# Pinned buffer homes and a later sink-key copy in a windowed-attention and feed-forward kernel

## The chip, the cores and the metric

The kernel runs on one core of one Trainium2 chip. The metric is the device time of one launch in microseconds (us). Each kernel was run several times; the text gives medians and ranges. Medians and ranges take every run; ratios take the runs counted as fast (at most 1.5% above the fastest of their kernel). Engines are named as in the profile: PE is TensorE (PEld its weight loads), DVE is VectorE, ACT is ScalarE, POOL is GpSimd, SP is SyncE.

## The reference, cut to what matters

Four batches of attention (8 heads, 768 positions, head size 64) in which each query sees the first 4 positions (the "sinks") and a window of 128 positions; then a multiplicative feed-forward over all 3072 rows.

```python
keep = is_sink | in_window              # 4 sink keys, or the last 128 keys
a = softmax(where(keep, q @ k.T / 8, -1e9))
x = (a @ v) reshaped to (3072, 512)
out = ((x @ w1) * (x @ w2)) @ w3 @ w_out
```

## The kernel before: the parts that matter

Every per-batch buffer is declared for four batches, with two, three or four physical homes under one tag. Which home a batch gets is decided when the program is built, by what is free then.

```python
def per_batch(name, shape, bufs):
    return [inp.tile(shape, BF16, tag=name, bufs=bufs, name=f"{name}{b}") for b in range(B)]

qN = per_batch("qN", [P, NB, DM], 2)      # queries as loaded
kN = per_batch("kN", [P, NB, DM], 2)      # keys as loaded
vN = per_batch("vN", [P, NB, H, VS], 3)
qT = per_batch("qT", [P, NP, S], 2)       # queries transposed
kT = per_batch("kT", [P, NP, S], 2)       # keys transposed
ksbd = per_batch("ksbd", [P, 648], 4)     # the 4 sink keys of all heads, spread out
# ... (cut)
```

Batches 0 and 1 are transposed on TensorE, batches 2 and 3 by DMA (6 key tiles and 6 query tiles each, issued from SP). The sink keys are two tiny VectorE copies out of the first key tile, and the sink scores are a TensorE product that needs those copies and the transposed queries:

```python
def sink_keys(b):
    for e in range(2):
        hp = slice(64 * e, 64 * e + 64)
        kk = ksbd[b][hp, 4 * e:4 * e + 640].rearrange("p (r x) -> p r x", x=160)
        nc.vector.tensor_copy(kk[:, :, 0:4], kT[b][hp, :, 0:4])
    yield

def sink_scores(b, t):
    sp = ps_mm.tile([P, 256], FP32, tag="mm", name="sp")
    for r in range(NP):
        nc.tensor.matmul(sp[:], ksbd[b][:, r * P:(r + 1) * P], qT[b][:, r, t * 256:(t + 1) * 256],
                         start=(r == 0), stop=(r == NP - 1))
    yield
    # ... exponential on ScalarE (cut)
```

The program order of PE, ACT, DVE and SP is fixed by a small list scheduler in Python, run while the kernel is built. It has its own guesses of durations and of when loads and transposes land. The two entries that matter:

```python
if t == 0:
    qk0 = qk
    task(("sk", b), 0, sink_keys(b), [("dve", 0.2)], [qk0[0]])          # after the first key tile
    # ... (cut)
else:
    task(("ss", b, t), 2, sink_scores(b, t), [("pe", 0.5), ("act", 0.4)],
         qk + [("sk", b)], ring="mm")                                    # after queries and sink keys
```

Each engine then runs its list in order, and waits on semaphores where the guess was too early. The Trainium skill (Perfetto Trace Analysis, Per-engine timelines) says that the execution queues of ScalarE, VectorE and GpSimd are strictly first in, first out; the traces below agree for VectorE: while one copy waits 7.18 us, nothing behind it starts.

The softmax here doesn't subtract the row's maximum and nothing guards it: scores larger than these inputs give would overflow.

## Time and profile before

| | before |
|---|---|
| time, median of 3 (range) | 226.0 us (225.19 to 226.41) |
| span of the profiled run | 224.0 us |
| TensorE busy | 199.1 us (89%) |
| longest TensorE wait after the start | 6.7 us |
| mean granted TensorE clock | 0.962 |

From the page of the kernel before: the span, busy time by engine, and TensorE's busy tenths and granted clock (tenths of full speed) in 40 slices of 5.6 us.

```profile
span 224.0 us, 4640 instructions
PE 199.1 (89%) x1882; PEld 133.8 (60%) x1888; DVE 109.2 (49%) x258; ACT 110.4 (49%) x197; POOL 75.2 (34%) x97
...
PE   1386799999999999870999999999999999999993
...
PEclk9998879999999999996599999999999999999999
```

TensorE is full except at the start and in slices 17 to 19 (the digits 8, 7, 0), and in slices 19 and 20 the granted clock falls to 6 and 5 tenths. The list of waits of the kernel before says who waited for whom (total us, times, longest us):

```profile
POOL kN_89 L100 <- DMA qT_96<-qN_84: 10.2, 1, 10.2
...
DVE ksbd_113 L184 <- DMA kT_101<-kN_89: 7.2, 1, 7.2
...
PE pg L283 <- DVE xn L258: 6.7, 1, 6.7
...
PE sp L201 <- DMA qT_96<-qN_84: 0.9, 1, 0.9
```

Read from the bottom: TensorE stood 6.7 us for a VectorE normalisation; VectorE stood 7.2 us at batch 3's sink-key copy (ksbd_113) for the DMA transpose of batch 3's first key tile; and POOL stood 10.2 us before it could load batch 3's keys at all, because their buffer was still being read by batch 2's transposes (the list names the query transposes, which landed last; in the built program that load waits for batch 2's key transposes). In order of time, the instructions of VectorE and TensorE around it (start us, us, what, and the idle time before it):

```profile
97.27 0.55 DVE L230 TENSOR_TENSOR am<-ex,maskt 128x768 bf16<-128x768 bf16 x1
104.99 0.62 DVE L184 COPY ksbd_113<-kT_101 64x16 bf16<-64x16 bf16 x2 [7.18 <-DMA kT_101<-kN_89]
...
98.23 1.47 PE L283 MATMUL pg<-xT_103,w_sb 128*128 128x384 bf16 x8
106.34 1.46 PE L283 MATMUL pg<-xT_103,w_sb 128*128 128x384 bf16 x4 [6.65 <-DVE xn L258]
```

### The profile page before, as it was taken

To read this page: it belongs to the slowest core of one execution; us is meant where nothing else is said; L and a number is where in the kernel's file an instruction comes from. 1 tells how busy PE (TensorE), PEld (TensorE's weight loads), DVE (VectorE), ACT (ScalarE), POOL (GpSimd) and SP (SyncE) were. 2 spreads that over 40 slices of the span, in tenths; PEclk is the share of its full clock that TensorE was granted. 3 is DMA by queue.
4 is the path that set the end of the run, shared out by engine and by line. 5 is a ranking of instruction groups with operands and counts; after the bars stand their busy time and mean duration, and the time that the engine had idled before them with its cause. 6 is when DMAs were issued, how large, how long until landed. Compare 5 with 4: busy or idle time off the path is not lost.

```text
span 224.0 us, 4640 instructions
## 1 busy us (share of the span) xinstructions
PE 199.1 (89%) x1882; PEld 133.8 (60%) x1888; DVE 109.2 (49%) x258; ACT 110.4 (49%) x197; POOL 75.2 (34%) x97
## 2 busy tenths in 40 slices
PE   1386799999999999870999999999999999999993
PEld 1274478998888787540566654566665455654441
DVE  6127525737797887522567753377752024340000
ACT  2022435655757876650467756577742343433332
POOL 7995473789898640398000000000000000000000
PEclk9998879999999999996599999999999999999999
DMA  4999999999999999799990012300000420002333
GB/s 68 161 176 202 163 205 191 176 162 154 145 148 128 155 144 156 69 134 138 156 181 4 3 74 113 143 1 3 0 0 11 169 104 0 3 1 94 142 143 140
DMA packets 96710, 24.43 MB, mean 109 GB/s; under 512 B 88496, under 2 KB 92592, under 8 KB 96688
## 3 DMA queue, kind: packets, MB, share of 16 engines
q0 software_dynamic: 80176, 14.69, 82.2%
q1 hardware_dynamic: 16512, 9.44, 19.2%
q8 instruction: 15, 0.25, 0.4%
q14 instruction: 7, 0.06, 0.1%
HBM read 29.36 MB, written 6.29 MB: 159 GB/s over the span
## 4 chain that ended last, share of the span: by engine, by line
PE 69%; DMA 18%; POOL 7%; DVE 3%; issue 1%; SPq 1%; ACT 1%; POOLq 0%; ACTq 0%; DVEq 0%
PE pg L283 31%; PE po L322 18%; PE pw L312 6%; DMA kN_88<-in_k_dram 5%; PE av L252 4%; PE sc L221 4%; DMA qN_84<-in_q_dram 3%; DMA w_sb<-in_moe_w_dram 3%; DMA qT_96<-qN_84 3%; DMA kT_101<-kN_89 3%; PE xt L268 2%; PE sp L201 1%; PE tp L167 1%; POOL vN_92 L100 1%; POOL vN_90 L100 1%
## 5 line engine op out<-in xcount | busy, mean ns | idle before, releaser
L283 PEld LDWEIGHTS <-w_sb 128*128 128x128 bf16 x576 | 54.7, 100 | 33.8 <-DVE xn L258 7.0
L290 ACT COPY a_sb<-pg 128x384 f32<-128x384 f32 (+1 forms) x72 | 31.9, 445 | 42.0 <-PE pg L283 27.5
L226 ACT ACTIVATE ex<-sc 128x1024 bf16<-128x1024 f32 (+1 forms) x48 | 44.1, 954 | 13.2 <-PE sc L221 12.7
L230 DVE TENSOR_TENSOR am<-ex,maskt 128x1024 bf16<-128x1024 bf16 (+1 forms) x48 | 30.3, 644 | 13.6 <-ACT ex L226 13.0
L283 PE MATMUL pg<-xT_103,w_sb 128*128 128x384 bf16 x128 | 26.7, 347 | 6.7 <-DVE xn L258 6.7
L326 ACT COPY o_sb<-po 128x512 f32<-128x512 f32 x24 | 14.0, 585 | 28.0 <-PE po L322 28.0
L283 PE MATMUL pg<-xT_102,w_sb 128*128 128x256 bf16 x192 | 25.7, 281 | 0.3 <-ACT xT_102 L270 0.2
L312 PE MATMUL pw<-wo_sb,w3t 128*128 128x256 bf16 x128 | 19.0, 309 | 4.4 <-DMA wo_sb<-in_moe_w_out_dram 3.6
L283 PE MATMUL pg<-xT_104,w_sb 128*128 128x384 bf16 x128 | 22.6, 326 | 0.0
L258 DVE TENSOR_TENSOR xn<-av,rec 128x256 bf16<-128x256 f32 x48 | 20.4, 425 | 1.7
L283 PE MATMUL pg<-xT_105,w_sb 128*128 128x384 bf16 x128 | 21.0, 326 | 0.0
L287 DVE TENSOR_TENSOR ab_109<-a_sb,pg 128x384 bf16<-128x384 f32 x16 | 8.9, 555 | 22.3 <-PE pg L283 22.3
L252 PEld LDWEIGHTS <-am 128*128 128x128 bf16 x352 | 17.1, 98 | 3.2 <-DVE am L230 0.8
L312 PEld LDWEIGHTS <-w3t 128*128 128x128 bf16 x128 | 13.3, 109 | 7.9 <-issue 2.9
L315 ACT CAST w3o<-pw 128x256 bf16<-128x256 f32 x16 | 5.8, 378 | 19.3 <-PE pw L312 19.2
L256 DVE RECIPROCAL rec<-av 128x4 f32<-128x4 f32 x48 | 8.6, 178 | 12.8 <-PE av L252 12.5
L287 DVE TENSOR_TENSOR ab_106<-a_sb,pg 128x256 bf16<-128x256 f32 x24 | 9.9, 417 | 8.3 <-PE pg L283 6.0
L287 DVE TENSOR_TENSOR ab_107<-a_sb,pg 128x384 bf16<-128x384 f32 x16 | 8.8, 552 | 7.1 <-PE pg L283 4.0
L287 DVE TENSOR_TENSOR ab_108<-a_sb,pg 128x384 bf16<-128x384 f32 x16 | 8.8, 552 | 6.5 <-PE pg L283 5.1
L322 PE MATMUL po<-w3o,ab_106 128*128 128x512 bf16 x46 | 11.1, 379 | 0.1
L268 PE MATMUL xt<-ident,xn 128*128 128x128 bf16 x96 | 10.1, 226 | 1.2 <-DVE xn L258 0.8
L322 PE MATMUL po<-w3o,ab_108 128*128 128x512 bf16 x47 | 10.6, 379 | 0.1
(129 smaller groups left out, 265.4 us busy)
## 6 DMA issues: line engine op xcount, KB each, us to landing
out_dram<-o_sb SPq DMA_DIRECT2D x24, 256.0 KB, 2.0
w_sb<-in_moe_w_dram POOLq DMA_DIRECT2D x7, 512.0 KB, 10.0
wo_sb<-in_moe_w_out_dram POOLq DMA_DIRECT2D x2, 512.0 KB, 8.9
kN_86<-in_k_dram POOLq DMA_DIRECT2D x6, 128.0 KB, 11.2
qN_82<-in_q_dram POOLq DMA_DIRECT2D x6, 128.0 KB, 11.4
vN_90<-in_v_dram POOLq DMA_DIRECT2D x6, 128.0 KB, 10.1
kN_87<-in_k_dram POOLq DMA_DIRECT2D x6, 128.0 KB, 7.7
qN_83<-in_q_dram POOLq DMA_DIRECT2D x6, 128.0 KB, 7.2
```

Of the source, the lines that this page charges most:

```text
L221: nc.tensor.matmul(sc[:, e, c:c + n], kT[b][hp, r, kb * P:(kb + 1) * P], qT[b][hp, r, qb * P:qb * P + n], start=True, stop=True)
L226: nc.scalar.activation(ex[:, :, c0:], sc[:, :, c0:], ACTF.Exp, scale=scale)
L230: nc.vector.tensor_mul(am[:, :, c0:], ex[:, :, c0:], mk)
L252: nc.tensor.matmul(o, lhs, rhs, start=(n == 0), stop=(n == len(todo) - 1), skip_group_check=True)
L258: nc.vector.tensor_mul(xn[:], av[:, :, :, 0:D], rec[:].to_broadcast([P, 2, 2, D]))
L268: nc.tensor.transpose(xt[:, r, i, :], xn[:, i, :, :].rearrange("p e d -> p (e d)"), ident[:])
L283: nc.tensor.matmul(pg[:], w_sb[:, kk, dt * P:(dt + 1) * P], xT[b][:, kk, tk], start=(kk == 0), stop=(kk == NP - 1))
L287: nc.vector.tensor_mul(ab[b][:, dt, tk], gate_a.pop((b, c, dt))[:], pg[:])
L290: nc.scalar.copy(a_sb[:], pg[:])
L312: nc.tensor.matmul(po[:], w3T[i][:, j, :], wo_sb[:, j, cols], start=(j == 0), stop=(j == KFF - 1))
L322: nc.tensor.matmul(po[:], ab[b][:, kk, m * P:(m + 1) * P], w3o[:, kk, :], start=(kk == 0), stop=(kk == KFF - 1))
L326: nc.scalar.copy(o_sb[:], po[:])
```

## The change

Its intent: give each batch a fixed home (batch number modulo the number of homes), so that batch 3 does not have to wait for batch 2; and copy the sink keys only after the batch's second score tile, so that the copy does not stand in VectorE's way.

```diff
     def per_batch(name, shape, bufs):
-        return [inp.tile(shape, BF16, tag=name, bufs=bufs, name=f"{name}{b}") for b in range(B)]
+        return [inp.tile(shape, BF16, tag=f"{name}{b % bufs}", bufs=1, name=f"{name}_{b}")
+                for b in range(B)]
...
-                task(("sk", b), 0, sink_keys(b), [("dve", 0.2)], [qk0[0]])
+                task(("sk", b), 0, sink_keys(b), [("dve", 0.2)], [("sc", b, 1, 0)])
```

What the built programs show of it. The addresses of kN for batches 0 to 3 go from 82336, 88480, 82336, 82336 to 82336, 88480, 82336, 88480 (qN in the same way); so before, batch 3 shared batch 2's home. The sink scores of a batch may only be scheduled after its copy, so they move later on TensorE too. Counted in summed matmul time ahead of them (an estimate: each matmul costed with its start-to-start time at full clock in the trace of before, such as 0.109 us for 256 columns), batch 3's two sink-score products move from 82.7 and 87.9 us of work to 102.5 and 102.9 us.

## The prediction

> **What bounds the kernel now.** TensorE. The page's part 1 has it busy for 199.1 of 224.0 us, the chain of waits runs on it for 69%, and from 111 us to the end it has no idle worth naming (stretches table: 9.95 to 10.0 of every 10 us). So the time is TensorE's work plus its holes. The load-bound first 20 us are not touched. The one big hole is later: the list of waits has "PE pg <- DVE xn 6.7, 1". In order of time: batch 3's sink-key copy (ksbd_113) stands early in VectorE's program and waits 7.18 us, from 97.8 to 104.99, for the first transposed tile of batch 3's keys. Ready work stands behind it, so TensorE stops from 99.7 to 106.34.
>
> **The hole costs more than its length.** In the stretch 106 to 110 us the granted clock is 0.50. Four 384-column gate matmuls take 1.40 to 1.46 us there against 0.65 before; summed over the chain up to 114.4 us the slow clock costs about 3.2 us. The Trainium skill (TensorE: Matmul & The Clock Gate, Part 1) says that an idle window of about 3.4 us sends the clock to half and about 3.4 us of busy time restores it; this trace agrees (6.65 us idle, then about 6 us at 0.5).
>
> **What the change does.** No operation is added or removed, only moved.
> 1. Homes. Before, the addresses of the built program put qN and kN of batches 2 and 3 both in home 0; so batch 3's first key load waits on batch 2's DMA transposes ("POOL kN_89 <- DMA qT_96 10.2, 1", 83.0 to 93.21). Pinned, batch 3 takes batch 1's home, free by about 71 us. The loads go on at once behind the last two of vN, so batch 3's kN starts at about 87 us, not 93.2. From 72 to 83 us, beside transposes, a load was issued only every 1.6 us and took about 11 us to land, so I expect batch 3's first transposed tile at 99 to 104 us (estimate), not 105. Alone that would shorten the hole by 1 to 6 us.
> 2. Sink keys later. The copy now stands behind batch 3's second score tile. By summed matmul times that point comes at about 121 us, long after the tile lands under either home. This alone removes the hole.
>
> So the two parts overlap and do not add.
>
> **Sum.** Hole 6.65 + slow clock 3.2 = 9.9 us, all on the critical path. TensorE's 0.9 us wait for the last qT of batch 2 (at 92.5) stays about as it is: that product moves to about 94 us, but batch 3's loads now share the DMA with those transposes. Given back: about 0.8 us, as batch 2's copy now stands close before its product. Predicted: 226.0 - 9.9 + 0.8 = 216.9 us; range 214.5 to 220.5. Faster by over 2%: 0.93; within 2%: 0.06; slower: 0.01.
>
> **What would show it.** No VectorE wait on kT_101 over 1 us; no TensorE hole over 2 us after 30 us; granted clock 1.00 in every stretch after 40 us; "POOL kN <- qT" of 10 us gone; TensorE's busy time down by about 3 us; batch 1's 384-column gate group back from 347 to about 326 ns each.
>
> **What would make it wrong.** Batch 3's loads delay batch 2's last transposes by over 3 us, so that a new hole opens at the sink scores near 94 us; TensorE's new order waits on ScalarE or VectorE, both over 70% busy from 70 to 90 us; or the slow clock has another cause than the hole.

## The result, and the profile after

| | before | after |
|---|---|---|
| time, median (range) | 225.59 us (224.27 to 226.41), 4 runs | 214.64 us (214.44 to 216.62), 4 runs |
| ratio | | 0.954, 95% interval 0.9465 to 0.9614 |
| span of the profiled run | 224.0 us | 212.8 us |
| TensorE busy | 199.1 us | 195.3 us |
| mean granted clock | 0.962 | 0.989 |

A ratio here is the mean time of one kernel's fast runs over that of the other's of the same rounds, so it is not quite the ratio of the two medians. Repeated in two later sessions, the changed kernel gave 215.88 and 216.19 us with ratios 0.9553 and 0.9566.

The same rows of the page, for the changed kernel:

```profile
span 212.8 us, 4647 instructions
PE 195.3 (92%) x1888; PEld 131.8 (62%) x1888; DVE 109.5 (51%) x258; ACT 110.4 (52%) x197; POOL 75.0 (35%) x97
...
PE   0287799999998999999999999999999999999993
...
PEclk9999969999999999999999999999999999999998
```

The hole and the slow clock near 100 us are gone; the one slow slice left is at the start. The whole list of TensorE's waits in the changed kernel:

```profile
PE tp_232 L301 <- DMA w_sb<-in_moe_w_dram: 5.1, 1, 5.1
PE pw L313 <- DMA wo_sb<-in_moe_w_out_dram: 3.8, 1, 3.8
PE tp_304 L301 <- DMA w_sb<-in_moe_w_dram: 1.4, 1, 1.4
PE xt L269 <- DVE xn L259: 1.2, 3, 0.6
PE pw L313 <- DVE w3t L304: 0.8, 1, 0.8
PE pg L284 <- DVE kT_99 L171: 0.6, 1, 0.6
PE pg L284 <- ACT xT_102 L271: 0.5, 1, 0.5
PE av L253 <- DVE am L231: 0.4, 2, 0.2
```

The single waits over 0.8 us are load waits of the first 20 us. From the list of one source line and the order of time, the copy, and the sink scores of batches 2 and 3, of the changed kernel:

```profile
L185 DVE COPY ksbd_113<-kT_101 x2: 152/161/170, 124.9 to 125.1; 64x16 bf16<-64x16 bf16 x2
...
93.26 1.04 PE L202 MATMUL sp<-qT_96,ksbd_112 128*128 128x256 bf16 x8
...
125.88 1.04 PE L202 MATMUL sp<-qT_97,ksbd_113 128*128 128x256 bf16 x8
```

The copy runs at 124.9 us, and nobody waits on either side of it. Batch 3's sink scores run at 125.88 us; in the kernel before they ran at 117.1 and 122.4 us, in spite of the hole.

Where 11.2 us of span went: the hole, 6.65; the slow clock after it, about 3.1 (next paragraph); the wait for the last qT of batch 2, 0.9; together 10.65. The other 0.5 us or so was gained earlier: at the first score of batch 2, before stood at 89.32 us with 65.7 us of summed work done, after at 89.61 us with 66.5 us done: 0.8 us more work in 0.3 us more time, so about half a microsecond ahead.

The slow clock in the kernel before, in four stretches chosen so that their borders fall where the clock changed (busy us of PE, PEld, DVE, ACT, POOL, each with its count; then the granted clock, DMA share and GB/s):

```profile
98.91:102.32 3.41, 0.78 (x5) 0.27 (x3) 0.00 (x0) 0.48 (x1) 3.41 (x5) 1.00 2.09 141
102.32:105.73 3.41, 0.00 (x0) 0.00 (x0) 0.69 (x3) 0.00 (x0) 3.12 (x4) 0.50 2.07 135
105.73:109.15 3.42, 2.81 (x23) 1.67 (x24) 2.53 (x7) 0.91 (x2) 0.00 (x0) 0.50 1.99 155
109.15:112.56 3.41, 3.41 (x14) 1.81 (x14) 1.76 (x3) 1.83 (x3) 0.00 (x0) 0.50 1.65 155
```

TensorE worked 2.81 + 3.41 = 6.22 us at half clock, so half of that, 3.1 us, is what the slow clock cost in this execution (an estimate). The Trainium skill (TensorE: Matmul & The Clock Gate, Part 1) has the clock decided in free-running windows of 3413 ns; the trace agrees: the clock was at half for 10.24 us, three such windows.

### The profile page after: what moved, and what is told of

The parts are those of the page before. It is cut to its first block, busy times and chain, and to the rows that moved or that the text cites. A ratio compares the mean times of both kernels' runs of the same rounds, so it can differ in the third digit from the quotient of the medians.

```text
span 212.8 us, 4647 instructions
## 1 busy us (share of the span) xinstructions
PE 195.3 (92%) x1888; PEld 131.8 (62%) x1888; DVE 109.5 (51%) x258; ACT 110.4 (52%) x197; POOL 75.0 (35%) x97
## 4 chain that ended last, share of the span: by engine, by line
PE 86%; POOL 5%; DMA 3%; DVE 3%; issue 1%; ACT 1%; POOLq 0%; ACTq 0%; DVEq 0%
PE pg L284 41%; PE po L323 20%; PE av L253 7%; PE sc L222 6%; PE pw L313 6%; DMA w_sb<-in_moe_w_dram 3%; PE xt L269 3%; PE sp L202 2%; PE tp L168 1%; POOL vN_90 L101 1%; POOL qN_82 L101 1%; DVE xn L259 1%; POOL kN_86 L101 1%; DVE am L231 1%; POOL w_sb L108 1%
## 5 line engine op out<-in xcount | busy, mean ns | idle before, releaser
L284 PE MATMUL pg<-xT_102,w_sb 128*128 128x256 bf16 x192 | 26.6, 285 | 1.1 <-DVE kT_99 L171 0.6
L284 PE MATMUL pg<-xT_103,w_sb 128*128 128x384 bf16 x128 | 23.8, 326 | 0.0
L284 PE MATMUL pg<-xT_104,w_sb 128*128 128x384 bf16 x128 | 23.0, 326 | 0.0
L313 PE MATMUL pw<-wo_sb,w3t 128*128 128x256 bf16 x128 | 17.3, 291 | 4.6 <-DMA wo_sb<-in_moe_w_out_dram 3.8
L284 PE MATMUL pg<-xT_105,w_sb 128*128 128x384 bf16 x128 | 21.0, 326 | 0.0
L288 DVE TENSOR_TENSOR ab_109<-a_sb,pg 128x384 bf16<-128x384 f32 x16 | 8.9, 555 | 22.3 <-PE pg L284 22.3
L313 PEld LDWEIGHTS <-w3t 128*128 128x128 bf16 x128 | 12.5, 103 | 7.4 <-issue 3.1
L288 DVE TENSOR_TENSOR ab_108<-a_sb,pg 128x384 bf16<-128x384 f32 x16 | 8.8, 552 | 5.8 <-PE pg L284 5.4
L323 PE MATMUL po<-w3o,ab_106 128*128 128x512 bf16 x48 | 11.4, 380 | 0.0
L323 PE MATMUL po<-w3o,ab_107 128*128 128x512 bf16 x48 | 10.7, 379 | 0.0
L323 PE MATMUL po<-w3o,ab_108 128*128 128x512 bf16 x48 | 10.7, 379 | 0.0
```

The costliest lines, as they stand in the source:

```text
L284: nc.tensor.matmul(pg[:], w_sb[:, kk, dt * P:(dt + 1) * P], xT[b][:, kk, tk], start=(kk == 0), stop=(kk == NP - 1))
L288: nc.vector.tensor_mul(ab[b][:, dt, tk], gate_a.pop((b, c, dt))[:], pg[:])
L313: nc.tensor.matmul(po[:], w3T[i][:, j, :], wo_sb[:, j, cols], start=(j == 0), stop=(j == KFF - 1))
L323: nc.tensor.matmul(po[:], ab[b][:, kk, m * P:(m + 1) * P], w3o[:, kk, :], start=(kk == 0), stop=(kk == KFF - 1))
```

## The experiments

Each experiment edits the kernel before, unless it says otherwise. The kernels of one session share the runs of the kernel before.

### One part at a time: homes or copies

`late_only` keeps the homes as before and takes the second half of the diff alone. `homes_only` takes the first half alone. `late_b3_only` keeps the homes and moves only batch 3's copy:

```diff
-task(("sk", b), 0, sink_keys(b), [("dve", 0.2)], [qk0[0]])
+task(("sk", b), 0, sink_keys(b), [("dve", 0.2)],
+     [("sc", b, 1, 0)] if b == 3 else [qk0[0]])
```

The changed kernel ran with them, as yardstick: 

> The changed kernel once more, as the yardstick on the same chip as the next three. All theories: about 214.6 us against about 225.6 us of before, ratio about 0.953; no TensorE hole over 1 us after 30 us.

It measured 215.88 us, ratio 0.9553 (0.9518 to 0.9588).

For the late copies alone: 

> Only the sink-key copies moved later, homes as before (batch 3's qN and kN still in batch 2's home, so their loads still wait about 10 us and start near 93 us). Theory (the late copy alone removes the hole): 214 to 216 us, within 0.5% of the full change, no VectorE wait on kT_101, granted clock 1.00 after 40 us. Rival (the homes bring the gain, by earlier loads): most of it is lost, 220 to 226 us, with TensorE waiting for batch 3's transposes near 105 to 120 us.

Measured 214.88 us, ratio 0.9526 (0.9489 to 0.9562), not to be told from the full change. Its list of waits still has the home's wait, longer than ever, and its row of the stretches table shows a full TensorE through the place of the hole:

```profile
POOL kN L100 <- DMA qT<-qN: 12.1, 1, 12.1
...
100.00:106.00 6.00, 6.00 (x67) 3.90 (x66) 3.97 (x11) 4.25 (x8) 6.00 (x8) 1.00 2.28 146
```

So a 12 us wait of POOL costs nothing once nobody stands early at what it loads. The late copies bring the whole gain.

For the homes alone: 

> Only the homes pinned; sink-key copies stay early. Theory: batch 3's first key transpose is issued at about 95.5 us instead of 98.7 and lands near 102, so VectorE's wait is about 4 us instead of 7.2 and TensorE's hole about 3.5 us instead of 6.65: 222 to 223 us if the clock still drops, 219 to 220 us if the shorter hole keeps it at full. Rival (homes bring the gain): 215 to 217 us.

Measured 223.73 us, ratio 0.9913 (0.9878 to 0.9948). From its waits and stretches:

```profile
DVE ksbd L185 <- DMA kT<-kN: 5.1, 1, 5.1
PE pg L284 <- DVE xn L259: 4.3, 1, 4.3
PE sp L202 <- DMA qT<-qN: 1.9, 1, 1.9
...
101.40:104.80 3.40, 0.05 (x1) 0.05 (x2) 1.04 (x5) 0.00 (x0) 0.00 (x0) 1.00 1.98 137
104.80:108.20 3.40, 3.40 (x25) 1.93 (x26) 1.89 (x5) 1.57 (x3) 0.00 (x0) 0.50 1.76 157
108.20:111.60 3.40, 3.40 (x32) 2.20 (x30) 2.27 (x5) 2.30 (x4) 0.00 (x0) 1.00 1.49 147
```

The homes alone gain about 0.9%. They shorten the hole from 6.65 to 4.28 us and the slow clock to one window instead of three. But the transposes of batch 3 only start at 96.11 us instead of 98.66, though the loads start 6.4 us earlier (86.81 against 93.21). In the changed kernel those loads run beside batch 2's transposes; the median time from issue to landing of kN_89 is 9.4 us there, against 5.9 us before. And the wait for batch 2's last qT grew from 0.9 to 1.9 us in this profile.

For batch 3's copy alone: 

> Homes as before, and only batch 3's copy moved later; those of batches 0 to 2 stay early. Theory (one copy is the whole cause): the hole and the slow clock after it go, TensorE's 0.9 us wait for the last qT of batch 2 stays: 215 to 216.5 us. Rival (the reordering for all batches brings a good part): 218 us or more.

Measured 217.36 us (216.73 to 218.5), ratio 0.9637 (0.9594 to 0.9679): one copy brings most, not all, and the median lies 0.9 us above what I had expected. The profile names a wait that I had not: TensorE at the sink-value product of batch 3 (vp), which met vN before it had landed.

```profile
89.93 0.57 PE L191 MATMUL vp<-vN,sel 128*128 128x64 bf16 x8 [2.06 <-DMA vN<-in_v_dram]
...
86.60:90.00 3.40, 1.34 (x20) 0.65 (x18) 1.99 (x6) 0.81 (x1) 0.00 (x0) 1.00 2.03 117
90.00:93.42 3.42, 3.42 (x23) 2.08 (x24) 0.00 (x0) 2.25 (x4) 0.00 (x0) 0.50 1.29 126
```

A hole of 2.06 us was enough for a window of half clock, 1.7 us more. But this wait is not new with the edit: up to vp, TensorE's order is the same as in the kernel before, which shows no such wait. What differs is when TensorE gets there: at 87.87 us here, without a slow window after 20 us, and at 89.75 us in the profile of before, with two. The profiles of `keep_warm` (arrival 88.60 us, wait 2.36 us) and `scores_later` (87.39, 1.83), below, have the wait too; `copy_later` and `scores_later_warm`, with the same order, arrive after 90.8 us and do not wait.

Which other copy makes the rest? `late_b23_only` moves those of batches 2 and 3 (`if b >= 2` in the same edit). 

> Homes as before, copies of batches 2 and 3 moved later, those of 0 and 1 early. Theory (what moving only batch 3's copy left over is batch 2's part: with the early copy of batch 2 its sink scores and the sink-value product of batch 3 stand about 2 us of work earlier on TensorE and meet data that has not landed): as the full change, 214.5 to 216 us, no wait of TensorE on vN or qT. Rival (it was batches 0 and 1): as moving only batch 3's copy, about 217.4 us.

Measured 215.01 us, ratio 0.9526 (0.9478 to 0.9575), and no TensorE wait on vN in the list:

```profile
89.96 0.40 PE L191 MATMUL vp<-vN,sel 128*128 128x64 bf16 x8
```

The copies of batches 0 and 1 need not move. With batch 2's copy late, TensorE has batch 2's first sink scores 6.3 us of work later (69.5 against 63.2) and vp 0.9 us later (67.0 against 66.1). That batch 2's copy makes the rest is shown; how much of it is vp's wait, and how much its place, was not taken apart.

### Filling the hole

If the slow clock follows from the idle, useless work in the hole should keep it away. `keep_warm` computes the last gate group ahead of the hole ten times over; the first matmul of each pass restarts the sum, so the result stays right.

```diff
-        for kk in range(NP):
+        again = 9 if (b, c, dt, half) == (1, 0, 6, 1) else 0
+        for kk in list(range(NP)) * (1 + again):
             nc.tensor.matmul(pg[:], w_sb[:, kk, dt * P:(dt + 1) * P], xT[b][:, kk, tk],
                              start=(kk == 0), stop=(kk == NP - 1))
```

> The kernel before, hole and all, but the last gate group ahead of the hole is computed ten times over (36 extra 384-column matmuls into the same tile, about 5.9 us of otherwise idle TensorE, same result). Theory (the slow clock follows from the idle, and costs about 3.2 us on top of the hole): the granted clock stays at 1.00 after the hole, TensorE resumes at about the same 106 us, and the time falls by about 3 us to 222.5 us. Rival (the slow clock has another cause, such as the loads and transposes then under way, or a fixed schedule of the throttle): the clock still drops to 0.5 at about 103 us, and the time stays at 225.6 us or rises.

Measured 228.3 us, ratio 1.0108 (1.007 to 1.0145): within 2%, but the interval lies above 1, where I had expected 3 us less. The clock after the hole did what the theory says, but the time did not:

```profile
90.96 0.41 PE L191 MATMUL vp<-vN,sel 128*128 128x64 bf16 x8 [2.36 <-DMA vN<-in_v_dram]
...
100.04 7.97 PE L284 MATMUL pg<-xT,w_sb 128*128 128x384 bf16 x48
...
104.00:106.00 2.00, 2.00 (x14) 1.22 (x13) 1.86 (x6) 0.00 (x0) 2.00 (x4) 1.00 2.16 149
...
119.28 1.01 PE L201 MATMUL sp<-qT,ksbd 128*128 128x256 bf16 x4 [4.08 <-DMA qT<-qN]
```

The clock stays at 1.00 from 96 us until the second hole. (The wait at vp and the window of half clock behind it come ahead of the filler, which cannot have caused them; TensorE reached the filler 1.8 us later than the same place in the profile of before. This is the profile of the slowest of the six runs.) In this profile the copy was released at 103.98 us, so the filler, which ran to about 107 us, overshot by some 2 us. And then TensorE, no longer held up, ran into a second hole of 4.08 us: batch 3's first sink scores need its transposed queries, which had not landed. In the kernel before there was no such wait in the profile, since the first hole and the slow clock had delayed TensorE enough: it reached that product at 117.12 us, against 115.2 us here. This fells the simple story. Behind the hole that the profile shows, another seems to stand, hidden by it; if so, the late copies must have removed both. The next runs test it.

### Copy or scores: which has to move?

Two kernels part the two movements that the late copy makes. `copy_later` moves batch 3's copy on VectorE just far enough to be out of the way, while its sink scores keep their place on TensorE. `scores_later` leaves the copy early, and moves only the scores. They were run on another chip.

```diff
 # copy_later
-task(("sk", b), 0, sink_keys(b), [("dve", 0.2)], [qk0[0]])
+task(("sk", b), 0, sink_keys(b), [("dve", 0.2)],
+     [qk0[0]] + ([("sc", 2, 1, 1)] if b == 3 else []))
 # scores_later
-     qk + [("sk", b)], ring="mm")
+     qk + [("sk", b)] + ([("sc", 3, 1, 0)] if b == 3 else []), ring="mm")
```

> Homes as before; batch 3's sink-key copy moved later on VectorE only so far (behind batch 2's sixth score tile) that the sink scores of batch 3 keep their old place on TensorE (about 82.4 and 87.2 us of summed matmul work, against 82.7 and 87.9). New theory, after keep_warm (late copies help because TensorE's sink scores of batch 3 move later with them; at their old place they meet the transposed queries, which land near 117 and 122 us): VectorE's wait on kT falls under 2 us, but TensorE gets a wait on qT of 5 to 9 us before the first sink score, and the time stays at 223.5 to 226 us. Rival (my prediction: VectorE's blocked queue is the whole cause): 215 to 218 us.

Measured 227.2 us, ratio 1.0105 (1.0033 to 1.0176): no gain (verdict: unclear, with the interval above 1). From the order of time of VectorE and of TensorE, and the stretches:

```profile
104.76 0.88 DVE L184 COPY ksbd<-kT 64x16 bf16<-64x16 bf16 x2
...
116.20 1.01 PE L201 MATMUL sp<-qT,ksbd 128*128 128x256 bf16 x4 [8.42 <-DMA qT<-qN]
...
106.91:110.32 3.41, 0.86 (x6) 0.29 (x3) 2.22 (x4) 1.66 (x3) 0.00 (x0) 1.00 1.88 133
110.32:113.73 3.41, 0.00 (x0) 0.00 (x0) 0.00 (x0) 0.00 (x0) 0.00 (x0) 0.50 1.68 149
```

VectorE's wait is gone (the copy starts with no idle before it), and the hole has moved: it now begins 8 us later, lasts 8.42 us and stands at the sink scores, with the slow clock in and after it.

> Homes as before; the copy stays early on VectorE, but the sink scores of batch 3 are held on TensorE until behind batch 3's second score tile (100.5 us of summed work). Both theories: VectorE's wait of 4 to 7 us, TensorE's hole and the slow clock stay, 224 to 226 us. If it fell below 220 us, the blocked VectorE queue would not be a cause at all.

Measured 223.72 us, ratio 0.9915 (0.9832 to 0.9998; verdict: unclear), a little below what I had expected; the hole of 6.0 us behind VectorE's copy is still in its list of waits. So the copy alone gains nothing and the scores alone about 1%, while both together (late_b3_only, on the other chip) are worth 3.6%. With the runs counted as slow kept in, the means give 1.006 for `copy_later` and 0.991 for `scores_later`: the same reading.

Not run: either movement with pinned homes. In the changed kernel the fourth query transpose of batch 3, which the first sink scores need, was issued only 0.6 us earlier than in `copy_later` (107.87 against 108.45 us), so I would expect the second hole there too; that is not shown.

With the scores out of the way, the fill can show what the clock costs. `scores_later_warm` is `scores_later` with the filler of `keep_warm`, at six extra passes. 

> As scores_later, plus 24 extra matmuls in the hole (the gate group ahead of it computed seven times, about 3.9 us, same result), so TensorE idles under 3 us there. With the wait on qT out of the way the cost of the slow clock can show. Theory: clock 1.00 after the hole, 1.5 to 3.5 us less than scores_later, 221.5 to 224 us. Rival (filling only moves the loss elsewhere, as in keep_warm): no faster than scores_later.

Measured 221.27 us, ratio 0.9806 (0.9716 to 0.9896). The end of the hole and the stretches 102 to 110 us of `scores_later`, then of the filled kernel:

```profile
106.13 1.46 PE L283 MATMUL pg<-xT,w_sb 128*128 128x384 bf16 x4 [6.04 <-DVE xn L258]
...
102.00:106.00 4.00, 0.00 (x0) 0.00 (x0) 1.01 (x5) 0.00 (x0) 4.00 (x5) 0.63 2.02 138
106.00:110.00 4.00, 3.87 (x27) 2.18 (x28) 2.07 (x6) 1.98 (x3) 0.09 (x1) 0.52 1.98 147
```

```profile
104.46 0.82 PE L284 MATMUL pg<-xT,w_sb 128*128 128x384 bf16 x4 [0.66 <-DVE xn L258]
...
102.00:106.00 4.00, 3.23 (x32) 1.74 (x31) 2.60 (x9) 0.48 (x1) 3.30 (x4) 1.00 2.49 154
106.00:110.00 4.00, 4.00 (x42) 2.55 (x37) 2.67 (x6) 3.29 (x5) 0.00 (x0) 1.00 1.75 157
```

The clock is plain: 1.00 against 0.63 and 0.52. The time is not: the medians differ by 2.45 us, of the size that I expected, but the two intervals overlap (0.9832 to 0.9896), and in these profiles the clock is not the only difference. The copy was also released 1.6 us earlier in the filled kernel (103.29 against 104.91 us), and only the unfilled one has the wait at vp. TensorE worked 3.72 us at half clock in and after this hole of `scores_later`, so I estimate the clock's part at 1.9 us; as a gain in time it is not shown.

### A try at the rest, inconclusive

In the changed kernel one slow stretch is left, between 20 and 33 us, and its place differs from run to run. `warm_start` is the changed kernel with useless matmuls in the load waits ahead of it:

```diff
+        if i == 2:                                          # ahead of the third block of w3
+            warm = ps_mm.tile([P, 512], FP32, tag="mm", name="warm")
+            for _ in range(6):
+                nc.tensor.matmul(warm[:], ident[:], w3_sb[:, 0, 0:512], start=True, stop=True)
...
+        for _ in range(14 if (i, n) == (0, 0) else 0):      # ahead of the first fold product
+            nc.tensor.matmul(po[:], ident[:], w3_sb[:, 0, 0:DM // 2], start=True, stop=True)
```

> The changed kernel plus 20 matmuls whose result nobody reads, in TensorE's load waits at the start (14 of 256 columns in the wait for w_out at 6 to 10 us, 6 of 512 columns in the wait for w3 at 17 to 19 us). If the slow clock between 20 and 33 us, which differs from run to run, follows from TensorE's idle at the start, the granted clock there is 1.00 in every run and the time is 213 to 214.5 us with less spread. If the start is bound by the loads alone: same as the changed kernel or up to 1 us slower.

> The changed kernel as yardstick for the three other runs on this chip: about 215 us, 214.4 to 216.6, the spread following the granted clock of the run.

Measured 215.15 us (214.69 to 215.57), ratio 0.9518 (0.9486 to 0.955), beside 216.19 us (215.44 to 218.97), ratio 0.9566 (0.9523 to 0.9609), for the changed kernel. The intervals overlap, and the slow stretch is still there in its profile: the clock averages 0.58 from 26 to 28 us. So it is not shown to be a gain, and no version was found that clearly beats the changed kernel. `late_only` and `late_b23_only` equal it with a smaller edit.

## Why the prediction was right or wrong, point by point

- **The time.** Predicted 216.9 us, 214.5 to 220.5, faster by over 2%; measured 214.64 us. Right, just inside the low end of the range. That it held for this edit is in part luck: of the two things that the edit moves on TensorE's path, I had reasoned about one (see "Sink keys later").
- **The hole and the clock, 9.9 us.** Right in size: 6.65 us of hole and about 3.1 us of slow clock (3.2 predicted) left the critical path. All the signs named in advance came: no VectorE wait on kT_101, no TensorE hole over 0.6 us after 30 us, clock 1.00 after 40 us, TensorE busy 3.8 us less, batch 1's 384-column gates at 326 ns instead of 347.
- **The homes.** Right: "alone that would shorten the hole by 1 to 6 us", measured 2.4 us (6.65 to 4.28). The first load began at 85.41 us in the changed kernel and at 86.81 us with the homes alone (87 predicted), and with the homes alone the copy was released at 103.68 us (99 to 104 predicted). That the two parts do not add is right as well: 0.9% alone, nothing on top of the late copies.
- **"Sink keys later. [...] This alone removes the hole."** True of the edit as written; not true of the reason given for it, the copy's place on VectorE. `copy_later` unblocks VectorE and gains nothing; `scores_later` moves the scores and gains about 1%. The edit works since it moves the copy and also batch 3's sink scores, about 20 us of work later on TensorE. At their old place the scores meet queries that have not landed (8.42 us of wait in `copy_later`). I had seen the scores move and given it no weight; I had not seen that second hole, because the profile of before cannot show a wait that another wait hides.
- **"Given back: about 0.8 us", and the wait of 0.9 us that "stays about as it is".** Both wrong in size: nothing was given back and the wait went, as the sink scores of batch 2 ran at 93.26 us without waiting. Together 1.7 us of the 2.3 us by which the median came out lower; another 0.4 us is that I started from 226.0 us and the kernel before measured 225.59. The sum should not be pressed: in the two later sessions the changed kernel came out at 215.88 and 216.19 us, 1.0 and 0.7 us below the prediction. The risk behind the term is real: with the homes alone that wait was 1.9 us, and in the profile of `warm_start`, the changed kernel's order with a filled start, it is back with 0.9 us.
- **Not foreseen.** Half a microsecond was gained before 90 us. Run-to-run differences of the slow stretch near 20 to 33 us are of that size, so no cause is claimed.

## What to carry to other kernels

Before counting a hole as gain, ask what the stalled engine will meet next when it arrives there earlier: walk down its list to the next operand that comes by DMA, and compare its landing time with the new arrival. An instruction that is put early on an in-order engine "because it is small" can cost as much as its operand is late, if work that others need stands behind it, and its consumers should be moved with it; here the two moved together because of one dependence in the scheduler, and either alone was worth about 1% or nothing. A long wait on a loading engine (12 us here) may cost nothing, so test it alone before repairing it. And a wait that one profile shows and another of the same order does not may only tell when the engine arrived there: compare the arrival times before blaming the edit.

## What the Trainium skill lacked or had wrong

- TensorE: Matmul & The Clock Gate, Part 1 says that the clock falls after at least one idle window of about 3.4 us. Here a window that was not idle sufficed: with batch 3's copy alone moved, TensorE was busy for 1.34 of 3.40 us (one hole of 2.06 us) and the next window ran at half clock. Busy time alone does not decide it: with the homes alone, a window with 1.49 us busy (91.16 to 94.57 us) was followed by one at full clock, and in `scores_later` one with 1.58 us busy (85.96 to 89.37 us) by one at half. The free-running window itself is confirmed: slow times of 10.24 us and 3.4 us in different runs, three windows and one.
- The same page says that about 3.4 us of busy time restores the clock. That agrees with the traces where the window was full. In the kernel before, a window with 2.81 of 3.42 us busy was followed by one more at half clock, while earlier in the same trace one with 2.99 of 3.41 us (27.23 to 30.64 us) was enough. So a hole's cost in clock depends on where it falls by more than a microsecond (estimates, half of the work done at half clock): about 1.9 us for the hole of 6.04 us in `scores_later`, which ended 0.3 us before a window's border, against 3.1 us for that of 6.65 us here.
- DMA: Bandwidth & Descriptors (Latency and other measured facts) gives the bandwidth of DMA transposes; a time from issue to landing for a tile of this size, beside running loads, was not found in the skill. Here a 128x512 tile of 2-byte elements was issued from SP in about 1.2 us and landed after a median of 7.1 to 7.6 us in the changed kernel; that latency is part of both holes.
